# Adding the recurrent state on TensorE for four chunks, and a ScalarE copy moved behind eight others

## The chip, the cores and the metric

The kernel runs on one core of one Trainium2 chip. A core has five engines that work through their own queues in order and meet only at semaphores: TensorE (PE in the rows, its weight loads are PEld), VectorE (DVE), ScalarE (ACT), GpSimd (POOL) and SyncE (SP), which here only issues DMA transfers. Matmul results go to PSUM, which is divided into banks; everything else lies in SBUF. The metric is the device time of one execution in microseconds (us), lower is better.

## The reference, cut to what matters

Three stages follow each other. The first is a linear-attention recurrence per batch and head, the second a feed-forward layer with a squared ReLU, the third a mixture of eight experts, of which each token uses two. Only the recurrence is touched:

```python
for t in range(S):                       # S = 768, D = 48, 4 batches x 8 heads
    kt, vt, rt = (k[:, :, t], v[:, :, t], r[:, :, t])
    cur = np.einsum('bhd,bhe->bhde', u[None] * kt, vt)
    y[:, :, t] = np.einsum('bhd,bhde->bhe', rt, state + cur)
    state = w[None, :, :, None] * state + np.einsum('bhd,bhe->bhde', kt, vt)
...
x = y as (3072 tokens, 384)
g = np.maximum(x @ w_in, 0.0) ** 2       # w_in 384 x 2048
x = g @ w_out                            # then the router and the experts
```

## The kernel before, in words

The recurrence is done in 24 chunks of 128 tokens, six to a batch; chunk q has index c = q % 6 within its batch. With c = 0 the state is zero. Per chunk the work is cut into steps, each a short function:

- `pre` multiplies r, k and u on GpSimd (tile `ra`), and scales the keys (`kp`, L412). `p_tr` transposes r or k on TensorE (L444) and evacuates the result (`rT`, `kT`).
- `pre2` sums the diagonal terms (`dg`, L418, VectorE), copies part of the values into a zero-padded tile (`vx`, L421), and lays the diagonals out (`am`): below chunk 8 by eight ScalarE instructions, one per head (L425).
- `p_a` forms the 128 x 128 products of r and k (L464, two PSUM banks) and copies them under a mask over `am` (L468, VectorE).
- `p_y 0` adds the state's part of the output (L482 with `Z`), `p_y 1` the rest (L482 with `am`); `p_x` turns the finished output into the two operands `x1h` and `x1l` of the feed-forward layer.
- `p_kv` forms the chunk's key-value products in one bank (L508, 16 small matmuls) and carries the state on. The state tile `Z` has two halves of 48 partitions, rows 0 to 47 and 64 to 111, handled one after the other. For c > 0 VectorE adds the old half to the bank's half (L515) and GpSimd multiplies the sum by the decay `wmid` (L516). Both old and new `Z` exist, in two alternating buffers.

The feed-forward layer takes blocks of 512 tokens, four chunks: `mm1` (L545), the activation on ScalarE (`gsplit`), and `mm2` (L576), 16 of each per block. Its weights arrive as 64-bit words and are converted on the chip in three steps (`conv_w1` L273 on ScalarE, `conv_w2` L280 to L292 on VectorE, `conv_w3` L302 on ScalarE and L303 on GpSimd).

The order is written out by hand. The table `HEAD` lists the steps for chunks 0 to 3 and the first conversions; everything before the first `mm1` comes from it. `warm n` in it is n transposes on TensorE whose results nobody reads. From then on the steps of the next four chunks stand in numbered slots between `mm1` and `mm2` (tables `CHUNKS`, `CONV_AT`); chunk 4 falls into the first slots of block 0. Each engine gets its instructions in the order in which these steps are called. The waits between engines are put in by the framework from the tiles that instructions read and write.

The constant `TPB` is 4, so `q <= TPB` and c > 0 together are chunks 1 to 4, the second to fifth.

Of the kernel before, what the change touches and what calls it, by code (L numbers as in the profile page):

```python
# [93 lines left out]
def body(ctx, tc, r, k, v, w, u, w_in, w_out, w_gate, w_noise, noise, w1, w2, out):  # L94
    nc = tc.nc
    B, H, S, D = r.shape
# [11 lines left out]
    TPB = BLK // P  # L108
# [51 lines left out]
    ident = consts.tile([P, P], F32, name="ident")  # L160
# [11 lines left out]
    def bank(tag="att", bufs=3):  # L172
        return ps.tile([P, 512], F32, name=tag, tag=tag, bufs=bufs)
# [147 lines left out]
    pb = bank()  # L321
# [43 lines left out]
    Z = [at.tile([P, HP, 2 * D], F32, name=f"Z{i}") for i in range(2)]  # L365
# [38 lines left out]
    def pairs(q):  # L404
        return L[q]["v"].rearrange("p (a s) d -> p a (s d)", s=2)

    def ends(q):
        t = vx[q % 2].rearrange("p a s x -> p (a s x)")
        return bass.AP(tensor=t.tensor, offset=t.offset, ap=[t.ap[0], [64, HP], [48, 2], [1, 16]])
# [4 lines left out]
    def pre2(q):  # L414
        a, l = A[q], L[q]
        t = a["rk"]
        dg = at.tile([P, H], F32, name="dg", bufs=2)
        nc.vector.tensor_reduce(dg, t, axis=AX.X, op=OP.add)  # L418

        own = nc.scalar.copy if q <= TPB else nc.gpsimd.tensor_copy  # L420
        own(ends(q), pairs(q)[:, :, 32:64].rearrange("p a (s x) -> p a s x", s=2))  # L421
        a["am"] = at.tile([P, H, P], F32, name="am", tag="am", bufs=2)
        if q < OWN_ACT:
            for h in range(H):
                nc.scalar.activation(a["am"][:, h, :], ident, AF.Copy, scale=dg[:, h:h + 1])  # L425
        else:
            nc.gpsimd.tensor_mul(a["am"], ident[:, None, :].to_broadcast([P, H, P]),
                                 dg[:, :, None].to_broadcast([P, H, P]))


    def p_tr(q, which, *tag):
# [67 lines left out]
    def p_kv(q, *tag):  # L499
        c = q % CPB  # L500
        if c == CPB - 1:
            return
        pb = bank(*tag)[:, :HP * D].rearrange("p (a d) -> p a d", d=D)
        kf = kp[q % 2].rearrange("p h x -> p (h x)")
        v = L[q]["v"]
        for hp in range(HP):
            for g in range(4):
                nc.tensor.matmul(pb[32 * g:32 * g + 32, hp, :], kf[:, hp * P + 32 * g:hp * P + 32 * g + 32],  # L508
                                 v[:, 2 * hp + g // 2, :], start=(hp == 0), stop=(hp == HP - 1), skip_group_check=True)
        for s in range(2):  # L510
            rows = slice(64 * s, 64 * s + D)
            zn = Z[(c + 1) % 2][rows, :, s * D:(s + 1) * D]
            w_ = wmid[rows, :, None].to_broadcast([D, HP, D])
            if c:
                nc.vector.tensor_add(zn, pb[rows], Z[c % 2][rows, :, s * D:(s + 1) * D])  # L515
                nc.gpsimd.tensor_mul(zn, zn, w_)  # L516
            else:
                nc.vector.tensor_mul(zn, pb[rows], w_)
# [536 lines left out]
    def run(pieces, n):  # L1055
        for p in pieces[:n]:
            p()
        del pieces[:n]

    AW = 3  # L1060
    steps = dict(spread=spread, warm=warm, p_tr=p_tr, pre=pre, tables=tables, pre_k=pre_k, load_w=load_w, p_a=p_a, pre2=pre2, p_kv=p_kv,
                 conv_w1=conv_w1, conv_w2=conv_w2, conv_w3=conv_w3, p_y=p_y, p_x=p_x, load=load)
    for step in HEAD:
# [4 lines left out]
    for j in range(NB):  # L1068
# [6 lines left out]
        if j + 1 < NB:  # L1075
            for i, at_ in enumerate(CHUNKS[min(j, 2)]):
                q = (j + 1) * TPB + i
                todo = [(pre, ()), (p_tr, "r"), (p_tr, "k"), (pre2, ()), (p_kv, ()), (p_a, ()), (p_y, (0,)), (p_y, (1,)),
                        (p_x, ())]
                for n, (fn, args) in zip(at_, todo):  # L1080
                    if q > TPB or fn not in (pre, p_tr):
                        put(n, fn, q, *args)
# [189 lines left out]
```

## Time and profile before

| | |
|---|---|
| median of 3 runs | 952.46 us (951.77 to 954.32) |
| the profiled execution | 953.81 us, its span 952.0 us |
| TensorE busy | 938.3 us, 99% of the span |
| VectorE busy | 533.7 us, 56% |
| ScalarE busy | 434.4 us, 46% |
| GpSimd busy | 345.8 us, 36% |

Busy shares are means over the whole span. The first 50 us, in which the steps of chunks 0 to 4 and the first weight conversions run, look different from the rest, and are the ones to read instruction by instruction. In the rows further below, the first number of a timeline row is the start in us from the span's start, the second how long the merged group took; a bracket at the end gives the idle time of that engine before it and what ended it.

### The profile page before, as it was taken

What the parts mean: (1) busy time and instruction counts of PE and PEld (TensorE: products, weight loads), DVE (VectorE), ACT (ScalarE), POOL (GpSimd) and SP (SyncE); (2) the same over time, 40 slices, a digit from 0 to 9 for tenths busy, and PEclk for the clock granted to TensorE, in tenths of its full rate; (3) what the DMA queues carried; (4) which work ended last, traced back from release to release, by engine and by line L of the source; (5) the groups of instructions that cost most, each with busy time, mean ns of one, the idle gap of its engine ahead of it and who ended that gap; (6) DMA issues with size and microseconds to landing.
All of it is one profiled execution on the core that took longest, in us unless ns stands there. A gap on an engine that the chain in (4) does not pass through costs nothing.

```text
span 952.0 us, 17757 instructions
## 1 busy us (share of the span) xinstructions
PE 938.3 (99%) x6845; PEld 805.0 (85%) x6845; DVE 533.7 (56%) x985; ACT 434.4 (46%) x798; POOL 345.8 (36%) x401
## 2 busy tenths in 40 slices
PE   9899999999999999999999999999999999999997
PEld 7677787778778778877888899999999898989987
DVE  8999757535835663583254564554545555456420
ACT  6766655334434434353555542443444444444321
POOL 6665353544563372545030353122121221212112
PEclk9999999999999999999999999999999999999999
DMA  8655379932444272342024357466645565645212
GB/s 182 161 163 164 99 192 301 245 108 64 118 121 106 55 189 57 106 108 77 1 101 98 103 137 183 108 135 135 130 97 114 121 117 109 117 94 111 33 21 37
DMA packets 193233, 112.32 MB, mean 118 GB/s; under 512 B 131777, under 2 KB 185698, under 8 KB 193122
## 3 DMA queue, kind: packets, MB, share of 16 engines
q1 hardware_dynamic: 181698, 91.03, 37.5%
q0 software_dynamic: 10624, 19.74, 11.2%
q8 instruction: 75, 1.23, 0.5%
q14 instruction: 36, 0.29, 0.1%
q10 hardware_dynamic: 800, 0.02, 0.0%
HBM read 74.64 MB, written 36.12 MB: 116 GB/s over the span
## 4 chain that ended last, share of the span: by engine, by line
PE 90%; DVE 5%; DMA 1%; issue 1%; ACT 1%; POOL 0%; POOLq 0%; ACTq 0%; DVEq 0%; SPq 0%
PE ph L545 20%; PE xo L576 19%; PE ph L866 19%; PE y L923 14%; PE y L954 4%; PE att L482 3%; PE ph L954 2%; PE att L464 2%; PE att L609 2%; PE y L866 2%; PE xo L570 1%; PE att L967 1%; DVE t L281 1%; PE att L508 1%; DVE am L468 1%
## 5 line engine op out<-in xcount | busy, mean ns | idle before, releaser
L934 POOL DMA_INDIRECT out<-yt,id x56 | 87.2, 1556 | 297.8 <-ACT yt L932 257.2
L560 DVE TENSOR_TENSOR gl<-g,gh 128x512 fp32r<-128x512 f32 x90 | 76.2, 846 | 134.9 <-ACT gh L558 131.4
L909 DVE SCALAR_TENSOR_TENSOR hl<-ph,hh 128x512 fp32r<-128x512 f32 (+1 forms) x112 | 66.9, 599 | 113.4 <-ACT hh L908 109.4
L550 ACT ACTIVATE rt<-ph 128x512 f32<-128x512 f32 x96 | 57.2, 596 | 157.9 <-PE ph L545 138.9
L545 PE MATMUL ph<-x1h,wih 128*128 128x512 f32 x288 | 119.3, 414 | 0.0
L866 PE MATMUL ph<-xh,w0h 128*128 128x512 f32 (+3 forms) x336 | 118.1, 352 | 0.0
L866 PE MATMUL ph<-xl,w0h 128*128 128x512 f32 (+3 forms) x336 | 116.2, 346 | 0.2 <-DVE xl L835 0.2
L866 PE MATMUL ph<-xh,w0l 128*128 128x512 f32 (+3 forms) x336 | 116.2, 346 | 0.0
L545 PE MATMUL ph<-x1h,wil 128*128 128x512 f32 x288 | 112.5, 391 | 0.0
L545 PE MATMUL ph<-x1l,wih 128*128 128x512 f32 x288 | 112.3, 391 | 0.0
L576 PE MATMUL xo<-gh,wol 128*128 128x512 f32 x270 | 106.2, 394 | 0.0
L908 ACT ACTIVATE hh<-ph 128x512 fp32r<-128x512 f32 (+1 forms) x112 | 58.7, 525 | 89.0 <-PE ph L866 82.1
L923 PE MATMUL y<-w1h,hh 128*128 128x384 f32 x256 | 85.7, 335 | 0.0
L923 PE MATMUL y<-w1l,hh 128*128 128x384 f32 x256 | 85.6, 334 | 0.0
L923 PE MATMUL y<-w1h,hl 128*128 128x384 f32 x256 | 85.6, 334 | 0.0
L737 POOL DMA_INDIRECT sent<-row,si x48 | 50.6, 1055 | 63.9 <-DVE gl L560 45.0
L576 PE MATMUL xo<-gh,woh 128*128 128x512 f32 x180 | 71.6, 398 | 0.0
L576 PE MATMUL xo<-gl,woh 128*128 128x512 f32 x180 | 70.2, 390 | 0.0
L866 PEld LDWEIGHTS ph<-xl,w0h 128*128 128x128 f32 x336 | 63.3, 189 | 7.7 <-DVE xl L835 0.9
L866 PEld LDWEIGHTS ph<-xh,w0l 128*128 128x128 f32 x336 | 63.2, 188 | 7.7
L866 PEld LDWEIGHTS ph<-xh,w0h 128*128 128x128 f32 x336 | 63.3, 188 | 7.0 <-ACT xh L834 0.3
L545 PEld LDWEIGHTS ph<-x1h,wih 128*128 128x128 f32 x288 | 54.0, 188 | 16.5 <-issue 3.3
(235 smaller groups left out, 2138.7 us busy)
## 6 DMA issues: line engine op xcount, KB each, us to landing
ws<-in_moe_w SPq DMA_DIRECT2D x128, 96.0 KB
ws<-in_moe_w SPq DMA_DIRECT2D x32, 384.0 KB
sent<-zero SPq DMA_DIRECT2D x8, 1375.5 KB
G<-sent SPq DMA_DIRECT2D x36, 192.0 KB
stg<-in_moe_w_in SPq DMA_DIRECT2D x8, 768.0 KB
stg<-in_moe_w_out SPq DMA_DIRECT2D x8, 768.0 KB
out<-zero SPq DMA_DIRECT2D x5, 960.0 KB
lv<-in_v SPq DMA_DIRECT2D x24, 192.0 KB
```

The costliest lines, as they stand in the source:

```text
L482: nc.tensor.matmul(pb[32 * n:32 * n + 32, d, :], x, y, skip_group_check=True, **kw)
L545: nc.tensor.matmul(ph, wt[qi][:, d, sl], xt[j][:, d, :], start=(n == 0), stop=(n == 3 * KD - 1))
L550: nc.scalar.activation(rt, ph, AF.Relu)
L560: nc.vector.tensor_tensor(gl, g, gh.bitcast(F32), op=OP.subtract)
L576: nc.tensor.matmul(XO[j][:, d, :], wt[qi][:, fo, sl], gt, start=(f == 0 and n == 0), stop=(f == NF - 1 and n == 2))
L737: st = nc.gpsimd.indirect_dma_start(out=sent, in_=s["row"][:, i, :], in_offset=None, out_offset=bass.IndirectOffsetOnAxis(ap=s["si"][:, i, ...
L866: nc.tensor.matmul(ph[:, c], wt[:, d, sl], xt[:, d, c], start=(m == 0), stop=(m == 3 * KD - 1))
L908: nc.scalar.activation(hh[:, :n], ph, AF.Relu)
L909: nc.vector.scalar_tensor_tensor(hl[:, :n], ph, 0.0, hh[:, :n].bitcast(F32), op0=OP.max, op1=OP.subtract)
L923: nc.tensor.matmul(py, ht[:, sl], wt[:, fo, :], start=(m == 0), stop=(m == 3 * NF2 - 1))
L934: st = nc.gpsimd.indirect_dma_start(out=out, in_=yt, in_offset=None, compute_op=OP.add, out_offset=bass.IndirectOffsetOnAxis(ap=IDX[e, un] ...
L954: nc.tensor.matmul(py[d][:, c], wt[:, fo, sl], ht[:, c], start=(m == 0), stop=(m == 3 * NF2 - 1))
```

## The change

In `pre2` the copy of the values stands behind the eight diagonal instructions and no longer ahead of them. In `p_kv`, for the second to fifth chunk, TensorE adds the old state's half to the bank by a matmul with the identity, and VectorE then multiplies the bank's half by the decay in one instruction. The addition on VectorE and the multiplication on GpSimd stand there no longer. Later chunks keep the old form.

```diff
@@ pre2
-        own = nc.scalar.copy if q <= TPB else nc.gpsimd.tensor_copy
-        own(ends(q), pairs(q)[:, :, 32:64].rearrange("p a (s x) -> p a s x", s=2))
         a["am"] = at.tile([P, H, P], F32, name="am", tag="am", bufs=2)
         ...
+        own = nc.scalar.copy if q <= TPB else nc.gpsimd.tensor_copy
+        own(ends(q), pairs(q)[:, :, 32:64].rearrange("p a (s x) -> p a s x", s=2))
@@ p_kv, in the loop for s in range(2)
-            if c:
+            if c and q <= TPB:
+                nc.tensor.matmul(pb[rows], ident[rows, rows], Z[c % 2][rows, :, s * D:(s + 1) * D],
+                                 start=False, stop=True, skip_group_check=True)
+                nc.vector.tensor_mul(zn, pb[rows], w_)
+            elif c:
                 nc.vector.tensor_add(zn, pb[rows], Z[c % 2][rows, :, s * D:(s + 1) * D])
                 nc.gpsimd.tensor_mul(zn, zn, w_)
```

In the changed kernel lines from `p_kv` on have numbers four higher, so that `mm1` is L549, and the new VectorE multiply is L517.

On TensorE, around `p_kv` of the second chunk, before (the names in brackets are the semaphores that an instruction waits for; DVE_49 is VectorE's):

```order
L444 MATMUL att<-ident,rp_95 112x128 x3
L508 MATMUL ph<-lv,kp_98 32x48 [waits DMAHW0_49]
L508 MATMUL ph<-lv,kp_98 32x48 x15
L444 MATMUL ph<-ident,kp_97 112x128 [waits DVE_49,Pool_49]
L444 MATMUL ph<-ident,kp_97 112x128 x3
L363 MATMUL xo<-ident 128x128 [waits PE_49]
```

The same place with the change:

```order
L508 MATMUL ph<-lv,kp_98 32x48 x15
L515 MATMUL ph<-Z_206,ident 48x192 [waits DVE_49,Pool_49]
L515 MATMUL ph<-Z_206,ident 48x192 [waits DVE_49]
L444 MATMUL ph<-ident,kp_97 112x128 [waits Pool_49]
L444 MATMUL ph<-ident,kp_97 112x128 x3
L363 MATMUL xo<-ident 128x128 [waits PE_49]
L363 MATMUL xo<-ident 128x128 x9
```

Two matmuls stand between the products and the transposes of the next chunk's keys, and each waits for VectorE.

On TensorE, at `p_kv` of the fifth chunk between the first two `mm1` of block 0, before:

```order
L508 MATMUL att<-lv,kp_97 32x48 [waits DMAHW7_49,PE_49]
L508 MATMUL att<-lv,kp_97 32x48 x15
L482 MATMUL att<-rT,Z_205 32x128 [waits PE_49,Pool_49]
L482 MATMUL att<-rT,Z_205 32x128 [waits Pool_49]
L482 MATMUL att<-rT,Z_205 32x128 x10
```

With the change:

```order
L508 MATMUL att<-lv,kp_97 32x48 x15
L515 MATMUL att<-Z_205,ident 48x192
L515 MATMUL att<-Z_205,ident 48x192 [waits DVE_49]
L482 MATMUL att<-rT,Z_205 32x128 [waits PE_49]
L482 MATMUL att<-rT,Z_205 32x128 x11
```

The first of the two matmuls waits for nothing, the second for VectorE, and the waits of the state's part of the output (L482) for GpSimd are gone.

On GpSimd, from the second chunk's `pre` to the third chunk's state, before:

```order
L400 TENSOR_TENSOR ra<-ra,ub 128x384 [waits Pool_49]
L516 TENSOR_TENSOR Z_205<-Z_205,wmid 48x4x48 [waits DVE_49]
L516 TENSOR_TENSOR Z_205<-Z_205,wmid 48x4x48 [waits DVE_49,Pool_49]
L412 TENSOR_TENSOR kp_98<-lk,tk 128x8x48 [waits DMAHW4_49,PE_49,Pool_49]
L399 TENSOR_TENSOR ra<-rp_96,lk 128x384 [waits DMAHW5_49]
```

With the change:

```order
L400 TENSOR_TENSOR ra<-ra,ub 128x384 [waits Pool_49]
L412 TENSOR_TENSOR kp_98<-lk,tk 128x8x48 [waits DMAHW4_49,DVE_49,PE_49]
L399 TENSOR_TENSOR ra<-rp_96,lk 128x384 [waits DMAHW5_49,DVE_49]
L400 TENSOR_TENSOR ra<-ra,ub 128x384 [waits Pool_49]
L303 TENSOR_TENSOR wil_132<-t_264,wih_124 128x768 [waits Activation_49]
```

The fourth chunk's key multiply (L412) no longer stands behind the two state multiplies.

## Rows read from the trace of the kernel before

**Rows 1.** Windows: length, busy (count) of PE, PEld, DVE, ACT, POOL; PEclk, DMA.
```profile
48.00:940.00 892.00, 890.53 (x6190) 765.57 (x6180) 490.67 (x911) 401.42 (x722) 311.21 (x355) 1.00 0.48 116
```
**Rows 2.** Timeline of TensorE, 15 to 25 us: `p_kv 1` to `p_a 2`.
```profile
15.63 0.55 PE L508 MATMUL ph<-lv,kp 128*32 128x48 f32 x32
16.11 0.65 PE L444 MATMUL ph<-ident,kp 128*112 128x128 f32 x4
...
17.77 1.74 PE L464 MATMUL att<-rT,kT 48*128 48x128 f32 x16
19.59 0.86 PE L482 MATMUL att<-rT,Z 112*32 112x128 f32 x24
...
21.40 0.30 PE L482 MATMUL att<-am,lv 128*32 128x128 f32 x1
...
22.30 0.52 PE L508 MATMUL ph<-lv,kp 128*32 128x48 f32 x32
22.75 0.65 PE L444 MATMUL ph<-ident,kp 128*112 128x128 f32 x4
23.33 1.16 PE L464 MATMUL att<-rT,kT 48*128 48x128 f32 x16
24.43 1.20 PE L363 MATMUL xo<-ident 128*128 128x128 f32 x9
```
**Rows 3.** Timeline of VectorE, 16 to 41 us, some of its instructions.
```profile
16.62 0.96 DVE L282 SCALAR_TENSOR_TENSOR t<-stg,t 128x768 int32<-128x768 int32 x1
...
18.22 0.73 DVE L515 TENSOR_TENSOR Z<-ph,Z 48x192 f32<-48x192 f32 x2
...
24.67 1.35 DVE L468 COPY_PREDICATED am<-mask,att 128x512 f32<-128x512 uint16 x2
...
28.31 1.65 DVE L282 SCALAR_TENSOR_TENSOR t<-stg,t 128x768 int32<-128x768 int32 x1
...
33.04 0.73 DVE L515 TENSOR_TENSOR Z<-ph,Z 48x192 f32<-48x192 f32 x2
33.81 0.56 DVE L528 TENSOR_TENSOR x1l<-att,x1h 128x384 fp32r<-128x384 f32 x1
...
40.07 0.73 DVE L515 TENSOR_TENSOR Z<-att,Z 48x192 f32<-48x192 f32 x2
```
**Rows 4.** Timeline of GpSimd, 18 to 30 us.
```profile
18.64 1.08 POOL L516 TENSOR_TENSOR Z<-Z,wmid 48x192 f32<-48x192 f32 x2 [2.47 <-DVE Z L515]
19.79 1.01 POOL L412 TENSOR_TENSOR kp<-lk,tk 128x384 f32<-128x384 f32 x1
...
27.81 1.32 POOL L399 TENSOR_TENSOR ra<-rp,lk 128x384 f32<-128x384 f32 x1
```
**Rows 5.** Timeline of TensorE, 30 to 49 us: `p_kv 3` to the fourth `mm1`.
```profile
30.65 0.55 PE L508 MATMUL ph<-lv,kp 128*32 128x48 f32 x32 [0.89 <-DVE am L468]
31.01 0.27 PE L482 MATMUL att<-am,lv 128*32 128x128 f32 x1
...
32.94 0.50 PE L545 MATMUL ph<-x1h,wih 128*128 128x512 f32 x1
...
35.31 0.55 PE L508 MATMUL att<-lv,kp 128*32 128x48 f32 x32
35.68 0.84 PE L482 MATMUL att<-rT,Z 112*32 112x128 f32 x24
...
40.95 1.13 PE L464 MATMUL att<-rT,kT 48*128 48x128 f32 x14 [1.75 <-DVE Z L515]
...
46.76 0.27 PE L482 MATMUL att<-am,lv 128*32 128x128 f32 x1 [0.37 <-DVE am L468]
...
48.38 0.50 PE L545 MATMUL ph<-x1h,wih 128*128 128x512 f32 x1
```
**Rows 6.** Timeline of TensorE: the small matmul that is nearest to the new one.
```profile
6.95 0.91 PE L356 MATMUL att<-us 1*128 1x384 f32 x2
```
**Rows 7.** Windows at the program's end, columns as in the first group.
```profile
948.00:950.00 2.00, 0.00 (x0) 0.00 (x0) 0.00 (x0) 0.00 (x0) 0.00 (x0) 0.58 0.84 102
```

## The prediction

> **What bounds the kernel now.** I read the windows first, then the timelines of the first 50 us. From 48 to 940 us TensorE is busy for 890.53 of 892.00 us at full clock [rows 1]: what it starts late at 48 us ends late by as much, and what the other engines lose there costs nothing. So the change is worth what it does to the start of the fourth `mm1`, at 48.38 [rows 5]. Before that, TensorE is not the bound. It waits 0.89, 1.75 and 0.37 us, each time for VectorE [rows 5], and part of what looks busy is the `warm` filler. VectorE works through a nearly unbroken queue in which the weight conversions stand between the steps of the chunks [rows 3]. TensorE runs ahead of it: `p_kv 1` starts at 15.63, and the VectorE instruction that uses its result at 18.22; `p_kv 4` starts at 35.31 and is used at 40.07 [rows 2, 3, 5]. So far this lead costs nothing, since nothing that follows `p_kv` on TensorE needs that VectorE instruction at once.
>
> **The change part by part: the new wait.** Per chunk, two matmuls are added, one for each half of the state. In the instruction order the first of them waits, in the fifth chunk, for nothing, and the second for VectorE. The old state cannot be the reason: both halves of it are written long before (for the fifth chunk by 33.77, ahead of 35.31 [rows 3, 5]). What lies between the two in the program is VectorE's multiply of the first half, which reads the same bank. So the framework lets the second half's matmul start only when VectorE has read the first half: matmul, multiply, matmul, multiply. TensorE's queue is in order. All that stands behind the second matmul (the next transposes, `warm`, `p_a`, `p_y`, `mm1`) now waits until VectorE comes to its multiply, which was the far end of TensorE's lead.
>
> The Trainium skill bears on whether the chip needs this ("PSUM — Partial Sum Buffer", section "PSUM bank collisions raise a hardware error"): engines must be kept apart by bank and 32-partition quadrant, and different quadrants of one bank may be used at once. By that rule the halves, at rows 0 and 64, need no wait on each other, and without one the result would be the second rival's; but the order shows a wait on VectorE in the program, and a semaphore is obeyed whether the chip needs it or not.
>
> **Prices.** The new matmul is fp32, 48 rows by 192 columns, and no row shows one. Nearest rows: one fp32 matmul with 384 columns (two passes, so x2) takes 0.91 us [rows 6]; the eight fp32 matmuls of `p_a` with 128 columns, which run in pairs, take 1.10 us or 0.14 each [rows 2]. The new one has half the columns of the wide one, so I take about half: 0.42 us until the next instruction starts and 0.5 until the result is there; the ends are 0.14 and 0.84. The multiply costs VectorE what the addition did, half of 0.73, or 0.36 us [rows 3]. A handover between engines is about 0.06 us: GpSimd started at 18.64, when VectorE's first half ended at 18.22 + 0.36 [rows 3, 4].
>
> **A second effect, on GpSimd.** Its two state multiplies per chunk go, eight in all, near 0.5 us each [rows 4]. None is on TensorE's path. But ahead of the fourth chunk's key multiply they held the queue: GpSimd stood idle 2.47 us for VectorE before 18.64, then did 1.01 us of key multiply at 19.79 [rows 4]. With them gone that multiply can start when `p_kv 1` is through, at about 16.2, just ahead of VectorE's L282 at 16.62 [rows 2, 3]. Beside GpSimd's L399 (27.81 to 29.13) the same L282 took 1.65 us in place of 0.96 and ended 0.83 after GpSimd did [rows 3, 4]. So L282 would end at 17.2 + 0.83, about 18.1 and not 17.6: 0.5 us later. The bound on the other side is zero, if VectorE comes first. The moved ScalarE copies (0.2 to 0.3 us each) shift ScalarE work by less than the lead that it has over VectorE and TensorE here; I cost them at nothing, and at 0.3 us if that lead is gone.
>
> **The sum.** Second chunk: multiply of the first half at 18.22 + 0.5 = 18.72, done 19.08, second matmul 19.14, next instruction 19.56. Before, that stood at 16.11. From there to `p_y 1` of this chunk was 5.29 us, but `p_a 1` in it took 1.82 (17.77 to 19.59), while waiting, against 1.10 undisturbed (23.33 to 24.43), so 4.57 remain [rows 2]: 24.13 in place of 21.40, 2.7 late. Third chunk: TensorE is now the late one, and the ping-pong itself costs 0.5 + 0.06 + 0.36 + 0.06 + 0.42 = 1.4: 4.1 late. VectorE's mask copy at 24.67 follows `p_a 2` [rows 2, 3], so VectorE is 4.1 late too. Fourth chunk: `p_kv 3` at 34.75; VectorE's multiply stands behind the mask copies, a conversion and a transposed operand, at 33.04 + 4.1 = 37.14; TensorE goes on 0.84 later at 37.98, not at 31.01 [rows 3, 5]: 7.0 late. Then `mm1` starts at 39.9, and with it x1l, which waits for the same ScalarE result and stood at 33.81: VectorE is 6.1 late. Fifth chunk: products at 39.9 + 2.37 = 42.3; multiply at 40.07 + 6.1 = 46.2; TensorE goes on at 47.0 with the state's part of the output, at 35.68 before [rows 3, 5], having stood still for about 3.5 us.
>
> From there the old waits are covered. Of the 12.70 us from 35.68 to 48.38 the waits of 1.75 and 0.37 go, and the broken `p_y` group needs 0.90 (21.40 to 22.30) and not 1.62 [rows 2, 5]: 9.9 us, so the fourth `mm1` starts at 56.9, 8.5 late. The stretches that I took over whole hold waits that fall otherwise: VectorE behind GpSimd (L282's 0.7 us above, and its like after 33.81) and TensorE groups that stopped midway for the mask. I take off 1.1 us for them, an estimate from those rows: 7.4 late.
>
> On the profiled execution (953.81 us, of which the span is 952.0) that makes 961.2; this execution was 1.35 above the median of the runs, and from the median 952.46 it makes 959.9, which I predict. The new matmul lies five times on the path, so its ends move this by -1.4 and +2.1, and GpSimd's lock by -0.5: 958.0 to 962.0 for this case alone.
>
> **The rivals.** *The clock falls in the stall.* At the end of the program, with no matmul left, the granted clock fell to 0.58 on the mean of 948 to 950 us [rows 7]. The longest wait of the kernel before is 1.75 us [rows 5], and the stall in the fifth chunk is twice as long. If the clock goes to its lower level (1.2 GHz), the state's part and the next `mm1`, 0.8 + 2.4 us at full speed [rows 2, 5], could take twice as long: 3 us more, 962.9. The Trainium skill says the same of gaps ("TensorE: Matmul & The Clock Gate", "Why this matters for your kernels"): an idle TensorE falls back to half rate and the next matmuls run slowly. For: length and place; against: one such stall, and after the wait of half that length the clock reads 1.00 from 48 us on [rows 1, 5].
>
> *Not slower: the second wait is met when it is reached.* If the second matmul waits only for the old state, TensorE never stops. Then four pairs cost it 4 x 2 x 0.42 = 3.4 us, mostly in the slack that VectorE leaves (0.89, 1.75 and 0.37 us [rows 5], and `warm` filler before that), and VectorE is relieved of GpSimd's blocks: L282's like, 0.2 to 0.7 us. That gives 952.0, and at the very best all three waits, 3.0 us, 949.5. It decides if in the new trace `p_tr` follows the products within a microsecond. Against it speaks the order: a wait on the second matmul alone.
>
> **How the numbers follow.** Forecast 0.70, clock 0.20, not slower 0.10. A measurement of this kernel tells about 0.3%, 2.9 us, from no change. The first two cases lie above that at all their ends: slower 0.90. Of the third I give 0.07 to no change and 0.03 to faster. The range 956.5 to 963.0 leaves out the third case and the tails of the others; it goes 1.5 below the forecast's own 958.0, as the taken-off waits could be larger.
>
> **What would show it.** Right: after `p_kv` two groups on L515 with idle time before the second, put down to VectorE's multiply, about 2.4 us in the second chunk, under 1 in the third, 2 in the fourth, 3.5 in the fifth; the fourth `mm1` near 55.8; nothing new behind it. The lock: L282 at 16.62 over 1.4 us long. The clock: PEclk under 1 between 43 and 52 us. Wrong: no idle time before the second L515, or a late fourth `mm1` whose delay is made up behind 48 us.

## The result

| | before, beside it | with the change |
|---|---|---|
| median | 952.96 us (951.77 to 954.32, 4 runs) | 963.75 us (963.25 to 963.99, 4 runs) |
| ratio, 95% interval | | 1.0111 [1.0098, 1.0123] |
| profiled execution, its span | 953.81, 952.0 us | 963.99, 962.2 us |

The kernel is 10.8 us slower, 0.75 us beyond the upper end of the predicted range. The direction and the new wait are as predicted; the clock fell behind two stalls, where the forecast had no such fall and the rival one.

The waits of TensorE from 12 to 60 us with the change: what it waited for, us in total, times, the longest.

```profile
PE ph L515 <- DVE Z L517: 5.3, 3, 3.0
PE att L515 <- DVE Z L517: 3.2, 1, 3.2
PE ph L508 <- DVE am L468: 0.3, 1, 0.3
...
```

All four second matmuls (L515) wait for VectorE's multiply (L517), 8.5 us together. The old waits of 1.75 and 0.37 us [rows 5] are gone and the one of 0.89 has shrunk to 0.34.

TensorE's timeline, at the four places and behind them:

```profile
7.58 0.91 PE L356 MATMUL att<-us 1*128 1x384 f32 x2
...
16.25 0.55 PE L508 MATMUL ph<-lv,kp 128*32 128x48 f32 x32
16.73 0.52 PE L515 MATMUL ph<-Z,ident 48*48 48x192 f32 x2
20.28 0.52 PE L515 MATMUL ph<-Z,ident 48*48 48x192 f32 x2 [3.03 <-DVE Z L517]
20.73 0.65 PE L444 MATMUL ph<-ident,kp 128*112 128x128 f32 x4
21.22 2.30 PE L363 MATMUL xo<-ident 128*128 128x128 f32 x10
...
29.22 0.52 PE L515 MATMUL ph<-Z,ident 48*48 48x192 f32 x2 [0.44 <-DVE Z L517]
29.68 0.65 PE L444 MATMUL ph<-ident,kp 128*112 128x128 f32 x4
...
39.81 0.52 PE L515 MATMUL ph<-Z,ident 48*48 48x192 f32 x2 [1.78 <-DVE Z L517]
...
48.47 0.83 PE L515 MATMUL att<-Z,ident 48*48 48x192 f32 x2 [3.23 <-DVE Z L517]
49.23 1.51 PE L482 MATMUL att<-rT,Z 112*32 112x128 f32 x24
50.66 0.80 PE L549 MATMUL ph<-x1h,wih 128*128 128x512 f32 x1
...
54.80 1.42 PE L464 MATMUL att<-rT,kT 48*128 48x128 f32 x16
...
61.49 0.50 PE L549 MATMUL ph<-x1h,wih 128*128 128x512 f32 x1
```

The last row is the fourth `mm1`, at 48.38 before [rows 5]: 13.1 us late. The steps below add up to 13.5; the other 0.4 is gained back in small pieces between them. The L356 group is 0.63 late from the start of this execution, before any changed matmul (6.95 before [rows 6]). Second chunk: L444 stands at 20.73, was at 16.11 [rows 2]: 4.0 more. Then the ten `warm` transposes take 2.2 us to the next group: 1.0 more. Third chunk: L444 at 29.68, was at 22.75 [rows 2]: 6.9 late in all, 1.4 more. Fourth chunk: the old wait ahead of it covers 0.5, the stall adds 2.9. Fifth: L482 at 49.23, was at 35.68 [rows 5]: 13.55 late, 4.6 more than just before. That group and the next `mm1` take 5.6 us up to L464, and 3.0 before: 2.5 more. The covered waits then give back 3.0.

The granted clock in these stretches (columns as in [rows 1]):

```profile
17.00:20.00 3.00, 0.25 (x2) 0.00 (x0) 2.93 (x4) 1.34 (x4) 3.00 (x3) 1.00 1.02 314
21.00:25.00 4.00, 4.00 (x30) 3.65 (x28) 1.22 (x3) 3.23 (x10) 0.18 (x1) 0.57 0.53 94
45.00:48.00 3.00, 0.24 (x2) 0.00 (x0) 2.93 (x5) 2.00 (x4) 0.00 (x0) 1.00 0.00 0
49.00:55.00 6.00, 6.00 (x36) 4.00 (x37) 3.42 (x5) 2.32 (x10) 0.90 (x1) 0.50 0.41 128
...
61.00:950.00 889.00, 889.00 (x6197) 765.43 (x6188) 495.85 (x910) 400.59 (x720) 309.09 (x353) 1.00 0.48 116
```

In both long stalls TensorE stands still at a full reading. After them it works at 0.57, on the mean of 21 to 25 us, and at 0.50, the lower level of 1.2 GHz. The last window matches [rows 1]: TensorE was idle 1.47 of 892 us before and not at all now. So a part of the 13.1 is made up after 61 us; the spans differ by 10.2. Of these 2.9 us about 0.9 go between 71 and 94 us, where TensorE before still waited for VectorE, and 1.5 near 200 us, where the profiled execution of the kernel before paused inside a group for no wait that the profile names:

```profile
200.61 0.42 PE L482 MATMUL att<-rT,Z 112*32 112x128 f32 x5 [1.03 <-issue]
```

This pause is no effect of the change: the traces of e5_second_only, e6_fifth_only, e7_held and e9_pair_later have one there too, of 0.7 to 1.0 us, and that of e2_copy_alone, which leaves TensorE's program as it was, has not.

VectorE in the second chunk:

```profile
15.26 1.04 DVE L280 TENSOR_SCALAR t<-t 128x768 f32<-128x768 f32 x1
...
17.61 1.64 DVE L282 SCALAR_TENSOR_TENSOR t<-stg,t 128x768 int32<-128x768 int32 x1
...
19.89 0.34 DVE L517 TENSOR_TENSOR Z<-ph,wmid 48x192 f32<-48x192 f32 x1
20.84 0.36 DVE L517 TENSOR_TENSOR Z<-ph,wmid 48x192 f32<-48x192 f32 x1 [0.61 <-PE ph L515]
```

Its L280 before:

```profile
14.63 0.68 DVE L280 TENSOR_SCALAR t<-t 128x768 f32<-128x768 f32 x1
```

Beside it GpSimd with the change:

```profile
17.12 1.31 POOL L412 TENSOR_TENSOR kp<-lk,tk 128x384 f32<-128x384 f32 x1
```

The key multiply L412, at 19.79 before [rows 4], now starts at 17.12, ahead of L282, which takes 1.64 us and not 0.96 [rows 3]. L280 takes 1.04 and not 0.68. And the ping-pong shows: L517 at 19.89, L515 at 20.28, the second L517 at 20.84 after an idle 0.61.

### The profile page after: what moved, and what is told of

It is laid out like the page before. It is cut to its first block, busy times and chain, and to the rows that moved or that the text cites. A ratio compares the mean times of both kernels' runs of the same rounds, so it can differ in the third digit from the quotient of the medians.

```text
span 962.2 us, 17772 instructions
## 1 busy us (share of the span) xinstructions
PE 944.4 (98%) x6861; PEld 809.2 (84%) x6861; DVE 539.9 (56%) x985; ACT 435.0 (45%) x798; POOL 340.0 (35%) x393
## 4 chain that ended last, share of the span: by engine, by line
PE 96%; DVE 2%; issue 1%; POOL 0%; ACT 0%; POOLq 0%; DVEq 0%; ACTq 0%
PE ph L549 21%; PE xo L580 19%; PE ph L870 19%; PE y L927 13%; PE y L958 5%; PE att L482 4%; PE att L464 3%; PE ph L958 2%; PE att L613 2%; PE y L870 2%; PE xo L574 2%; PE att L971 1%; PE att L508 1%; DVE t L281 0%; PE att L444 0%
## 5 line engine op out<-in xcount | busy, mean ns | idle before, releaser
L564 DVE TENSOR_TENSOR gl<-g,gh 128x512 fp32r<-128x512 f32 x90 | 83.6, 929 | 146.1 <-ACT gh L562 146.0
L549 PE MATMUL ph<-x1h,wih 128*128 128x512 f32 x288 | 120.0, 417 | 0.0
L549 PE MATMUL ph<-x1h,wil 128*128 128x512 f32 x288 | 113.2, 393 | 0.0
L549 PE MATMUL ph<-x1l,wih 128*128 128x512 f32 x288 | 112.9, 393 | 0.0
L549 PEld LDWEIGHTS ph<-x1h,wih 128*128 128x128 f32 x288 | 54.4, 189 | 16.6 <-issue 3.7
```

What stands on the lines that cost most here:

```text
L549: nc.tensor.matmul(ph, wt[qi][:, d, sl], xt[j][:, d, :], start=(n == 0), stop=(n == 3 * KD - 1))
L564: nc.vector.tensor_tensor(gl, g, gh.bitcast(F32), op=OP.subtract)
```

## The experiments

Each batch ran on one chip beside its own runs of the kernel before, whose medians were 952.57 (first four), 954.94 (next four) and 953.61 us (last two); compare by the ratio.

| run | median us | ratio [95%] |
|---|---|---|
| e1_pair | 953.02 | 1.0003 [0.9994, 1.0012] |
| e2_copy_alone | 952.45 | 1.0003 [0.9994, 1.0012] |
| e3_add_alone | 963.12 | 1.0108 [1.0093, 1.0123] |
| e4_filler | 960.38 | 1.0082 [1.0068, 1.0096] |
| e5_second_only | 961.32 | 1.0066 [1.0047, 1.0085] |
| e6_fifth_only | 958.78 | 1.0037 [1.0024, 1.0050] |
| e7_held | 964.87 | 1.0097 [1.0081, 1.0113] |
| e9_pair_later | 953.73 | 0.9987 [0.9978, 0.9996] |
| e10_filler_3 | 959.54 | 1.0062 [1.0049, 1.0076] |
| e11_middle | 957.25 | 1.0039 [1.0026, 1.0052] |

**e1_pair: the wait taken away.**

```diff
+        for s in range(2 if c and q <= TPB else 0):
+            rows = slice(64 * s, 64 * s + D)
+            nc.tensor.matmul(pb[rows], ident[rows, rows], Z[c % 2][rows, :, s * D:(s + 1) * D], ...)
         for s in range(2):
             ...
             if c and q <= TPB:
-                nc.tensor.matmul(pb[rows], ident[rows, rows], Z[c % 2][rows, :, s * D:(s + 1) * D], ...)
                 nc.vector.tensor_mul(zn, pb[rows], w_)
```

> Both identity matmuls of a chunk stand ahead of both VectorE multiplies, so that TensorE never waits for the first multiply; everything else is as in the changed kernel. My theory (the loss is that wait, with the clock that falls in it): TensorE has no idle time at these matmuls, the clock stays full, and the time is that of before, 951.5 to 954.0 us. Rival A (the added matmuls themselves are dear on TensorE): eight at 0.42 us or more stay, 956 or later. Rival B (GpSimd's key multiply, now early, delays VectorE): 0.5 to 1 us over before, and L282 near 17 us still takes 1.6 us.

It measured 953.02 us, no different from before. TensorE's waits from 12 to 60 us, and its window from 15 to 50:

```profile
PE att L464 <- DVE rT L449: 1.1, 1, 1.1
PE att L464 <- DVE Z L519: 0.7, 1, 0.7
PE ph L508 <- DVE am L468: 0.4, 1, 0.4
...
```

```profile
15.00:50.00 35.00, 32.29 (x521) 24.63 (x518) 33.63 (x46) 24.71 (x60) 18.42 (x13) 1.00 0.67 173
```

The same eight matmuls, with no wait at any of them and a full clock, cost nothing that can be measured. The loss is the order in which matmul and multiply were called, all of it but at most the 1.1 us that the interval leaves. Rival A falls. Of rival B the mark is there: L282 takes 1.65 us here too, and TensorE waits 1.1 us for rT (L449) behind it. Shorter waits later make up a part; the fourth `mm1` still starts at 49.46, 1.1 us late. In the time none of this is seen, but a loss of 0.5 to 1 us, as rival B has it, is not excluded by the interval.

**e2_copy_alone and e3_add_alone: the two parts apart.** The first is the kernel before with this, the second the changed kernel without it:

```diff
-        own(ends(q), pairs(q)[:, :, 32:64]...)     # ahead of the diagonals
         a["am"] = ...
+        own(ends(q), pairs(q)[:, :, 32:64]...)     # behind them
```

> The kernel before with only the ScalarE copy moved behind the diagonals; the state is added on VectorE and multiplied on GpSimd as before. My theory (the copy has no part in the loss): 952.0 to 954.0 us, the time of before. Rival (the copy, now in ScalarE's busy stretch, delays the weight conversion or the transposed keys): 1 us or more above before.

> The changed kernel with only the ScalarE copy put back ahead of the diagonals. My theory: 963 to 964.5 us, as the changed kernel. Rival (the copy has a part): at least 1 us lower.

They measured 952.45 and 963.12 us. The copy costs nothing that can be measured; the addition costs all.

**e4_filler: TensorE kept at work in the two long stalls.**

```diff
                 nc.tensor.matmul(pb[rows], ident[rows, rows], Z..., ...)
+                if s == 0 and q in (1, 4):
+                    warm(22 if q == 1 else 26)
                 nc.vector.tensor_mul(zn, pb[rows], w_)
```

> The changed kernel, with 22 (second chunk) and 26 (fifth chunk) idle transposes on TensorE between the first and the second identity matmul, so that TensorE works while it would stand still; the waits are the same and end at the same time. My theory (about 3.6 us of the loss is the clock that falls in these two stalls: ten transposes in 2.30 us for 1.26, and an mm1 group in 4.1 for 2.2): the granted clock stays at 1.00, the second matmuls start at the same times, and the time falls to 959.5 to 961 us. Rival (the slow groups have another cause, or the transposes do not keep the clock up): 963 to 964.5 us with a fallen clock after either stall.

It measured 960.38 us; by the ratios that is 0.29% or 2.8 us below the changed kernel. In both stalls and behind them the clock stays at 1.00. The stalls are about as long: from the first to the second matmul 3.9 and 3.4 us, with the change 3.55 and 3.75. In the fifth chunk it is the filler that held TensorE last: VectorE's multiply was done at 46.38, the second matmul started at 46.97. But in the profiled execution the clock fell after the fourth chunk's wait, where no filler stood. TensorE there (L444 takes 1.10 us and not 0.65), and the clock:

```profile
37.37 0.52 PE L515 MATMUL ph<-Z,ident 48*48 48x192 f32 x2 [1.79 <-DVE Z L519]
...
38.83 1.10 PE L444 MATMUL att<-ident,kp 128*112 128x128 f32 x4
```

```profile
39.00:40.00 1.00, 1.00 (x5) 1.00 (x5) 0.51 (x2) 1.00 (x2) 0.00 (x0) 0.50 1.04 395
```

With the change itself the wait of 1.78 us at the same place was followed by no fall.

**e10_filler_3: filler in the fourth chunk as well.**

```diff
-                if s == 0 and q in (1, 4):
-                    warm(22 if q == 1 else 26)
+                if s == 0 and q in (1, 3, 4):
+                    warm({1: 22, 3: 14, 4: 26}[q])
```

> As the run with idle transposes in two stalls, with 14 more between the two matmuls of the fourth chunk, where that run's clock fell after a wait of 1.79 us. My theory (what is left of the loss without a fallen clock is the stalls alone): clock 1.00 everywhere until the end of the program, 6.0 to 7.5 us above before, and 0.3 to 1.3 below the run with two fillers. Rival (the fall there was chance and rare, or transposes do not prevent it): no lower than that run, or a fall in another place.

```profile
14.00:24.00 10.00, 9.39 (x148) 7.64 (x141) 7.88 (x11) 6.59 (x22) 6.16 (x5) 1.00 0.83 181
...
38.00:42.00 4.00, 3.96 (x56) 2.87 (x60) 2.74 (x4) 1.74 (x4) 1.63 (x1) 1.00 1.01 283
```

```profile
56.05 0.50 PE L551 MATMUL ph<-x1h,wih 128*128 128x512 f32 x1
```

It measured 959.54 us: with the clock at 1.00 the stalls alone cost 5.9 us (0.62% [0.49, 0.76]), and against the change's 1.11% the fallen clock costs the other 0.49%, 4.7 us (2.9 to 6.5, an estimate from the two intervals). The last row is its fourth `mm1`, 7.7 us late where that of the change was 13.1 late. Against e4_filler its ratio is lower by 0.0020; the intervals overlap, so what the third filler is worth stays open.

**e5_second_only, e6_fifth_only, e11_middle: chunk by chunk.**

```diff
-            if c and q <= TPB:
+            if q == 1:            # e6_fifth_only: q == 4;  e11_middle: q in (2, 3)
                 nc.tensor.matmul(...)
```

> The changed kernel with the addition on TensorE for the second chunk alone; the other chunks add on VectorE and multiply on GpSimd as before. My theory (each chunk's loss is TensorE's stall until VectorE's first multiply, plus the fallen clock, minus old waits that it covers): 4.0 us of stall, about 1 of slow clock behind it, the old waits mostly kept because VectorE is late with TensorE: 956.5 to 958.5 us. Rival (the loss is one cost per added matmul, alike in all four chunks): a quarter of 11 us, about 955.5.

> The changed kernel with the addition on TensorE for the fifth chunk alone. My theory: the stall ends with VectorE's multiply near 40.4, TensorE goes on 5.2 us late, the clock falls and costs 2.5, and the old waits of 1.75, 0.37 and 0.2 us and the broken groups beside them, 3 to 4 us in all, are covered: 955.5 to 958 us. Rival (one cost per matmul): as for the second chunk alone, about 955.5, without a stall that differs from the other chunk's.

> The changed kernel with the addition on TensorE for the third and fourth chunk alone. My theory: the ping-pong costs 1.4 us in the third chunk, the stall in the fourth 2 to 3 us, of which the old waits behind it take back about 2: 1.5 to 4 us above before, so that the chunks apart (6.3 for the second, 3.6 for the fifth) add up to more than the 10.6 to 10.8 of all four. Rival (what each chunk costs is independent of the others): about 1 us above before, the rest of 10.8.

By their ratios they cost 6.3, 3.5 and 3.7 us, together 13.5, give or take 2.5 by their intervals, where the four chunks at once cost 10.6 to 10.8. One cost per matmul is out: a quarter of the loss lies below the interval of e5_second_only (4.5 to 8.1 us), and half of it above that of e11_middle (2.5 to 5.0). The second chunk missed its range: 961.32 us, where 956.5 to 958.5 was expected beside a kernel before of 952.5; beside its own, 954.94, the 6.3 us are 0.3 above the 6.0 of that upper end. Its clock had fallen by 20 us, within the wait. The four executions of e5_second_only spread from 959.09 to 962.51 us, and the slower ones have the lower mean clock (0.996, 0.994, 0.992, 0.991), so the clock is a part of this number. In e11_middle too it fell in the profiled execution, to 0.50 from 36 to 37 us, behind a wait of 1.78 us in the fourth chunk. Behind the second chunk's stall the old waits stand as before; the fifth chunk's stall covers them:

```profile
PE ph L515 <- DVE Z L517: 3.7, 1, 3.7
PE att L464 <- DVE Z L519: 1.7, 1, 1.7
PE ph L508 <- DVE am L468: 0.9, 1, 0.9
PE att L482 <- DVE am L468: 0.4, 1, 0.4
```

These are TensorE's waits in e5_second_only; in e6_fifth_only the new wait is the longest of all, and the 1.7 is not there:

```profile
PE att L515 <- DVE Z L517: 4.2, 1, 4.2
PE ph L508 <- DVE am L468: 0.9, 1, 0.9
PE att L464 <- DVE rT L449: 0.8, 1, 0.8
...
```

**e7_held: GpSimd's key multiply late again.**

```diff
                 nc.vector.tensor_mul(zn, pb[rows], w_)
+                nc.gpsimd.tensor_mul(zn, zn, C["ones"][rows, None, :D].to_broadcast([D, HP, D]))
```

> The changed kernel, in which GpSimd multiplies each new half of the state by one, in place, where it multiplied by the decay before, so that its key multiply for the fourth chunk again comes late. My theory (the early key multiply holds VectorE's L282 up): L282 near 17.5 us takes 0.96 and not 1.64 us, the second matmul of the second chunk starts 0.7 earlier after p_kv 1, and the time falls by 0.7, or by 1.8 if the shorter stall keeps the clock up: 961.8 to 963.2 us. Rival (GpSimd does not matter here): L282 stays at 1.6 us and the time at 963.7.

VectorE and then TensorE in the second chunk:

```profile
16.75 0.96 DVE L282 SCALAR_TENSOR_TENSOR t<-stg,t 128x768 int32<-128x768 int32 x1
```

```profile
15.67 0.52 PE L515 MATMUL ph<-Z,ident 48*48 48x192 f32 x2
18.74 0.87 PE L515 MATMUL ph<-Z,ident 48*48 48x192 f32 x2 [2.55 <-DVE Z L517]
```

L282 is back at 0.96 us, and from the first L515 to the second it is 3.07 us, with the change 3.55: 0.5 less. So GpSimd's early multiply does lengthen the stall. In the time this doesn't show: 1.0097 against 1.0111, the intervals overlap, and the clock fell in the shorter stall all the same (the second matmul takes 0.87 us for 0.52). On the time this run is inconclusive.

**e9_pair_later: a faster version.** As e1_pair, for the third to fifth chunk (`q in (2, 3, 4)`), with the ScalarE copy at its old place.

```diff
-        for s in range(2 if c and q <= TPB else 0):
+        for s in range(2 if q in (2, 3, 4) else 0):
```

> A try for a faster version: the addition on TensorE, both matmuls ahead of both multiplies, for the third to fifth chunk; the second chunk as before, so that GpSimd's key multiply stays late; the ScalarE copy where it was before. My theory: no stall on TensorE at the added matmuls, VectorE's conversions near 42 us rid of GpSimd's two multiplies there, 0.2 to 0.7 us earlier at the fourth mm1, within the spread of before: 951.5 to 953 us. Rival (the added matmuls cost what they take): up to 2 us above before.

It measured 953.73 us beside 954.94, a ratio of 0.9987 [0.9978, 0.9996]: 1.2 us faster than before, just clear of no change, and faster than the changed kernel by about 1.2%. Near 42 us VectorE runs without GpSimd's two multiplies in its way; first before, with GpSimd's row, then this run:

```profile
42.32 0.75 DVE L281 TENSOR_SCALAR t<-t 128x768 int32<-128x768 int32 x1
43.10 1.15 DVE L282 SCALAR_TENSOR_TENSOR t<-stg,t 128x768 int32<-128x768 int32 x1
41.83 1.61 POOL L516 TENSOR_TENSOR Z<-Z,wmid 48x192 f32<-48x192 f32 x2
```

```profile
41.99 0.56 DVE L281 TENSOR_SCALAR t<-t 128x768 int32<-128x768 int32 x1
42.58 0.96 DVE L282 SCALAR_TENSOR_TENSOR t<-stg,t 128x768 int32<-128x768 int32 x1
```

That this makes the 1.2 us is not shown, and its trace speaks against it. Here are the transposes of the second chunk, ahead of every changed matmul, and the fourth `mm1`; first before, then this run, with its own fourth `mm1` (before: 48.38 [rows 5]):

```profile
15.05 0.65 PE L444 MATMUL att<-ident,rp 128*112 128x128 f32 x4
```

```profile
14.56 0.65 PE L444 MATMUL att<-ident,rp 128*112 128x128 f32 x4
...
47.89 0.50 PE L551 MATMUL ph<-x1h,wih 128*128 128x512 f32 x1
```

The fourth `mm1` is 0.49 us earlier, as expected (0.2 to 0.7), but so was TensorE at 15 us: over the changed stretch the trace shows no gain. Where the 1.2 us come from stays open.

## Why the prediction was right in the mechanism and wrong in the size

- **The wait.** Right. "The framework lets the second half's matmul start only when VectorE has read the first half": all four second matmuls wait for L517, and calling the matmuls in pairs removes the loss, to within 1.1 us (e1_pair). Whether the chip would run the two halves without that wait, as the Trainium skill's "PSUM — Partial Sum Buffer" has it for different quadrants ("PSUM bank collisions raise a hardware error"), no run shows: e1_pair puts all matmuls ahead, it doesn't overlap them with the reads.
- **The terms.** Second chunk 3.45 predicted (16.11 to 19.56), 4.0 measured; VectorE's L282 took 0.68 more where I had 0.5, and its L280 0.36 more; why L280 did was not tried. Ping-pong in the third 1.4, measured 1.4. Fourth 2.9, measured 2.9. Fifth 4.3 (11.3 less 7.0), measured 4.6. My 0.42 us for the new matmul was near: 0.45 from the second L515 to the next group.
- **The sum without the clock.** Near. My sum put the fourth `mm1` 7.4 us late, 8.5 without the 1.1 us that I took off. In e10_filler_3, whose clock stayed at 1.00, it is 7.7 late. From the change's own trace, 13.1 less 0.63 of a late start and 3.5 of slow clock is 9.0. Whether the 1.1 us were right stays open between the two.
- **"Nothing new behind it", the rest is passed on one for one.** Wrong: the fourth `mm1` was 13.1 late and the end 10.2, and the last line of "what would show it" named just that as a failure. TensorE before was idle for 1.5 us behind 48 us [rows 1], after not at all. Of the 2.9 us about 0.9 are old waits behind 61 us that the late TensorE no longer meets; 1.5 are the pause near 200 us of one execution before, which has nothing to do with the change. About 0.5 were not traced to single groups.
- **The clock: the step that failed.** "Forecast 0.70, clock 0.20", and "one such stall". The sum put the fallen clock at nothing, and the rival priced one fall at 3 us. The second chunk's stall was 3.03 us by the profile and belonged with the fifth's 3.23; my own rows gave it 2.4. The clock fell behind both and cost 1.0 and 2.5 us in the trace; with TensorE kept at work the time drops by 2.8 (e4_filler) to 4.7 us (e10_filler_3). Without the fall the time would have been well inside my range: the stalls alone cost 5.9 us, and I had 7.4. With it the rival's 962.9 would have been the better forecast, and two falls lie beyond its price. The Trainium skill's "TensorE: Matmul & The Clock Gate" ("Why this matters for your kernels") warned of such gaps; the trace agrees for the stalls of 3.03 and 3.23 us, and e4_filler shows a fall after 1.79 us too.
- **The copy.** Right: nothing that can be measured (e2_copy_alone, e3_add_alone).
- **GpSimd's early multiply.** Right in kind and size: 0.5 us of stall predicted, 0.5 by e7_held; not visible in the time.

## What to carry to other kernels

When two engines share one PSUM bank, call all writes of the one before the first read of the other: a read between two writes makes the framework chain them, even on different partitions (whether it goes by the bank or by the tile, no run here tells), and the engine that ran ahead stops at the reader's queue. Look through the instruction order for a wait on the second of two equal instructions, and price it with the distance by which the one engine leads the other in the trace. Price every stall of some microseconds on TensorE twice, once for its length and once for the slower clock behind it.

## What the runs showed that was not expected

The granted clock also fell after waits far shorter than the two long ones, and not in each execution: after 1.79 us in e4_filler and 1.78 us in e11_middle and in e7_held, but not after 1.78 us with the change, nor after 2.48 us in the fifth chunk of e7_held. In e6_fifth_only it fell near 21 us, where of the change only the moved copy is in the program and TensorE had waited 0.22 and 0.76 us in the microseconds before:

```profile
15.00:20.00 5.00, 4.02 (x78) 3.15 (x68) 4.46 (x6) 4.44 (x13) 2.19 (x2) 1.00 0.88 227
20.00:22.00 2.00, 1.92 (x33) 1.64 (x37) 1.94 (x5) 0.37 (x2) 1.68 (x3) 0.77 1.19 202
22.00:24.00 2.00, 2.00 (x19) 1.61 (x12) 1.11 (x3) 2.00 (x9) 1.92 (x3) 0.50 0.16 32
```

Nor does the fall come at a fixed place in the wait: with the change the clock read 1.00 throughout both stalls and dropped only when TensorE was at work again, about 1.0 us after the end of the first stall and 0.1 us after that of the second; in e5_second_only it read 0.50 from 19 to 20 us, while TensorE still stood.
